# Scan and mixture of adapters on one core: tokens in 4 KB rows over pairs of chunks, transposes in 64-row tiles, a second set of banks in the tail

## The chip, the core and the metric

The kernel runs on one core of a Trainium2 chip. The core has five engines that run their own instruction streams side by side and wait for one another through semaphores: TensorE (PE in the profile; its weight loads are shown as PEld), VectorE (DVE), ScalarE (ACT), GpSimd (POOL) and SyncE (SP), which here only issues transfers. Sixteen DMA engines move data between the device memory and the core's SBUF. TensorE writes into PSUM, which has eight banks of 2 KB per partition; ACT and DVE copy from there. The metric is the device time of one execution in microseconds, the median of several runs.

## The reference

Two layers, one after the other. The first is a linear recurrence over 6400 time steps for 8 sequences of 128 features: `h = a[:, t] * h + b[:, t]`, each h is an output row. Its 51200 rows x then go through a mixture of 8 adapters of rank 16:

```
logits = x @ w_gate                       # 8 experts
topk = two largest; w = softmax over the two
delta[row] += w[row, k] * ((x[row] @ A[e]) @ B[e])   # for its two experts
return x + delta
```

Inputs a and b (26 MB each, fp32) are read once, and the output (26 MB) is written once.

## The kernel before

A *chunk* is 512 tokens; there are 100. In the loads, partition p of a chunk holds the four tokens 4p to 4p+3 (`J` = 4), so one partition's row of a transfer is 4 x 128 x 4 B = 2 KB. Loads bring two chunks at a time (`HC` = 2, 512 KB for a and as much for b, into one of six buffers each), stores take two chunks at a time too; the first four chunks are loaded singly and the last four stored singly.

For each chunk (`front`):

- A and B (L419): four fp32 transposes of a 128x128 tile each, through TensorE against `ident_f`, put a into the bank `pA` and b into one of the two banks `pB`, features on partitions, tokens along the free dimension. The four tokens of a partition go to every fourth column (`"d (p j) -> d j p"`).
- ae (L430): ACT copies pA to SBUF (`a_st`), since the scan may read only one operand from PSUM.
- sc (L442): DVE runs the recurrence over 512 tokens, `xT = a_st * state + pB`, fp16 out. Chunks hang together through the last column of the chunk before; a chunk in which a new sequence begins is done in two pieces.

The rest works in *units* of six blocks of 128 tokens (the last four units have four), 68 units in all (`zlogits` and `back`):

- Z (L462): six matmuls with xT blocks as weights give, per token, 128 adapter values and 8 logits, in the two banks `pZ`; ze (L468) on ACT copies them to `zl`.
- Gating (`gating`, L489 to L518), once for a group of four units (in the tail for groups of 2, 2, 1, 1, 1, 1 units): five small DVE instructions, two sigmoids on ACT and four small POOL instructions give the weights g.
- mu (L533 on POOL, L537 on DVE for the last two units, `MU_DVE` = 2): zw = zl * g, fp16.
- T (L543): six fp16 transposes of zw into the bank `pT`; te (L552 on DVE, for one unit in four L549 on ACT) copies them to `zwT`.
- D (L558, L559): per block two matmuls that add up in the two banks `pO`: x itself (xT against `ident_h`), then zwT against B. oe (L569) on ACT copies to the output buffer `outt` (72 blocks).
- st (L595): SP issues the store when all blocks of its chunks are copied.

So T of a unit waits for te of the unit before (one bank pT), and D waits for oe of the unit before (one pair pO).

The order of instructions on each engine is fixed when the program is made. `Program.schedule` plays a model of the engines with a duration for each operation (such as `0.109 * J` for A), rates for loads and stores (`LOAD_RATE`, `STORE_RATE`), a rank for each operation from `TEMPLATE` and a look-ahead `WINDOW` per engine, and takes, engine by engine, what can start first. `Program.waits` then gives each instruction the semaphore waits that its inputs and buffers need. All loads and stores but one go through SP's queue in the order so planned. WARM transposes on the identity (L359) fill PE in the first microseconds.

Of the kernel before, what the change touches and what calls it, by code (L numbers as in the profile page):

```python
# [10 lines left out]
PERIOD = 6  # L11
# [6 lines left out]
LOAD_RATE = 386e3  # L18
STORE_RATE = 420e3
# [4 lines left out]
WINDOW = {'pe': 22.339, 'act': 15.032, 'dve': 17.853, 'pool': 31.507, 'sp': 21.093}  # L24
# [5 lines left out]
MU_DVE = 2  # L30
WARM0 = 12
WARM = 34
LAST = 2
TEMPLATE = {
    "la": [-13.768, -11.488, -10.699],
    "lb": [-11.599, -10.876, -10.408],
    "A": [-8.739, -5.735, -4.61, -4.527, -4.01, -3.388],
    "B": [-0.753, -0.06, 2.522, 2.886, 3.39, 4.151],
    "ae": [6.378, 8.693, 8.757, 9.146, 10.126, 12.233],
    "sc": [11.891, 15.28, 15.373, 17.047, 17.106, 17.222],  # L40
    "Z": [8.614, 8.864, 13.261, 13.471],
    "ze": [17.232, 19.133, 19.801, 20.09],
    "g1": [13.208],
    "g2": [18.458],
    "g3": [3.74],
    "g4": [5.014],
    "g5": [35.276],
    "g6": [5.048],
    "w1": [11.688],
    "w2": [17.689],  # L50
    "p1": [18.712],
    "p2": [4.238],
    "p3": [33.725],
    "mu": [17.377, 18.243, 18.627, 23.065],
    "T": [19.784, 21.14, 23.513, 25.169],
    "te": [11.814, 12.075, 12.746, 13.615],
    "D": [22.711, 24.793, 26.772, 27.207],
    "oe": [23.268, 23.347, 25.158, 27.374],
    "st": [18.431, 19.751, 20.387],
    "ta": [11.3, 11.673, 14.3, 15.8],  # L60
    "md": [10.222, 11.5, 13.0, 14.5],
    "wu": [-0.392],
    "ch": [5.145],
# [146 lines left out]
def bass_associative_scan_2x2__then__mixture_of_adapters_kernel(  # L210
# [32 lines left out]
    GMAX = 4  # L243
    groups = []
# [14 lines left out]
    NX = 24  # L259
# [13 lines left out]
    with ExitStack() as stack:  # L273
# [19 lines left out]
        a_tm = sbuf("a_tm", [128, HC, J, D], F32, NL)  # L293
        b_tm = sbuf("b_tm", [128, HC, J, D], F32, NL)
        a_st = sbuf("a_st", [128, C], F32, NA)
        xT = sbuf("xT", [128, C], F16, NX)
# [17 lines left out]
        pB = psum("pB", [128, C], F32, 2)  # L314
# [59 lines left out]

        def xblock(b):
            return xT[b // J % NX].rearrange("d (p j) -> d j p", j=J)[:, b % J, :]

# [15 lines left out]

        def load(c, n):
# [3 lines left out]
            for o_l, o_t, key, tile, src in ((o_la, o_A, "la", a_tm, af), (o_lb, o_B, "lb", b_tm, bf)):  # L398
                q = "act" if c == 0 and key == "lb" else "sp"
                op = P.add(  # L400
                    q, f"{key}{c}", n * C * D * 4 / LOAD_RATE, get(o_t, HC * (p - NL) + HC - 1),
                    lambda tile=tile, src=src, q=q: eng[q].dma_start(
                        tile[sl][:, h : h + n, :, :],
                        src[r0 : r0 + n * C, :].rearrange("(h p j) d -> p h j d", p=128, j=J),
                    ),
                    (FIRST, "", 0) if c < 2 else (PERIOD * (c // PERIOD), key, c % PERIOD // 2), sem=dma_sem(f"{key}{sl}" if n == HC else f"{key}x{c % 4}"),
                )
                for k in range(n):
                    o_l[c + k] = op

        def front(c):
            sl = c // HC % NL
            r0 = rows[c]

            def trans(dst, src):
                def f():
                    dv = dst.rearrange("d (p j) -> d j p", j=J)
                    for j in range(J):
                        last = eng["pe"].transpose(dv[:, j, :], src[:, j, :], ident_f[:, :])  # L419
                    return last  # L420
                return f

            o_A[c] = P.add("pe", f"A{c}", 0.109 * J,
                           [(o_la[c], True), (o_id, True)] + get(o_ae, c - 1),
                           trans(pA[:, :], a_tm[sl][:, c % HC, :, :]), fr(c, "A"))
            o_B[c] = P.add("pe", f"B{c}", 0.109 * J,
                           [(o_lb[c], True), (o_id, True)] + get(o_sc, c - 2),
                           trans(pB[c % 2][:, :], b_tm[sl][:, c % HC, :, :]), fr(c, "B"))
# [3 lines left out]
            x = xT[c % NX]  # L432
# [3 lines left out]
            def scan():  # L436
                for s0, s1 in segs:
                    if (r0 + s0) % S == 0:
                        init = 0.0
                    else:  # L440
                        init = xT[(c - 1) % NX][:, C - 1 : C]
                    last = eng["dve"].tensor_tensor_scan(  # L442
                        out=x[:, s0:s1], data0=a_st[c % NA][:, s0:s1], data1=pB[c % 2][:, s0:s1],
# [6 lines left out]
                            + get(xlast, c % NX),  # L450
                            scan, fr(c, "sc"))

        def zlogits(u):
            b0, n = units[u]
            c1 = (b0 + n - 1) // J
# [66 lines left out]
        def back(gi, u):  # L522
# [7 lines left out]
            if u < NU - MU_DVE:  # L530
# [9 lines left out]

            def tr():
                for k in range(n):
                    last = eng["pe"].transpose(pT[:, k * 128 : k * 128 + 128], zw[w][:, k, :], ident_h[:, :])  # L543
                return last

            o_T[u] = P.add("pe", f"T{u}", 0.056 * n, [(o_mu[u], True), (o_ih, True)] + get(o_te, u - 1), tr, ba(gi, u, "T"))
            if te_act(u):
                o_te[u] = P.add("act", f"te{u}", 0.15 + 0.107 * n, [(o_T[u], True)] + get(o_D, u - NW),
                                lambda: eng["act"].copy(zwT[w][:, 0 : n * 128], pT[:, 0 : n * 128]), ba(gi, u, "ta"))  # L549
            else:  # L550
                o_te[u] = P.add("dve", f"te{u}", 0.14 + 0.0672 * n, [(o_T[u], True)] + get(o_D, u - NW),
                                lambda: eng["dve"].tensor_copy(zwT[w][:, 0 : n * 128], pT[:, 0 : n * 128]), ba(gi, u, "te"))  # L552

            def delta():
                for k in range(n):
                    o = k % (n // 2) * 128
                    dst = pO[:, k // (n // 2), o : o + 128]
# [131 lines left out]
```

## Time and profile before

| | |
|---|---|
| median of 3 runs | 208.79 us (208.51 to 209.43) |
| the profiled execution | 209.08 us; from its first to its last instruction (span) 206.9 us |
| granted TensorE clock, mean | 0.992 |
| busy, of the span | PE 94%, DVE 87%, ACT 83%, POOL 64% |
| moved by DMA | 79.17 MB, 383 GB/s over the span |
| the chain that ended last | 88% of it on PE |
| costliest groups | scan L442 120.3 us in 96, mu L533 96.3 us in 66, transposes L419 61.7 us (a) and 61.3 us (b) in 400 each, ae L430 60.5 us in 100 |

A line of an instruction group or of the timeline names the line of the kernel, the engine, the operation, and what is written and read; f16 and f32 are types. Matmuls overlap on PE: one is shown from its start to its end, and the next may start before that. The timeline joins neighbours of one kind (x4). In the table of stages, a row has the stretch in microseconds, its length, then busy time and number of instructions of PE, PEld, DVE, ACT and POOL, then the granted clock, the mean busy share of the 16 DMA engines, and GB/s.

### The profile page before, as it was taken

The numbers are of one execution on the slowest core, as the hardware profiler recorded it, in microseconds if no ns is written. First come the engines' busy times: TensorE is split into PE (matmuls) and PEld (weight loads), VectorE is DVE, ScalarE is ACT, GpSimd is POOL, SyncE is SP. The second block draws the span as 40 slices with busy tenths as digits, with TensorE's granted clock in tenths as the row PEclk, the third lists the DMA queues.
The fourth block names the chain that finished last, engine by engine and source line by source line (L and its number), as shares of the span: only waits on it lengthen the run. The fifth ranks groups of instructions, "written<-read, shape, count | busy, mean of one in ns | idle before, by whom it ended". The sixth has DMA issues, their size and how long they took to land.

```text
span 206.9 us, 6064 instructions
## 1 busy us (share of the span) xinstructions
PE 194.1 (94%) x2434; PEld 185.8 (90%) x2434; DVE 179.2 (87%) x266; ACT 172.5 (83%) x295; POOL 132.8 (64%) x156
## 2 busy tenths in 40 slices
PE   6988699999999999999999999999999999998762
PEld 6976589999999999999999999999999999997641
DVE  0379959999999999999999999999998989978871
ACT  2266949979999999999989898989998989898552
POOL 1000194868686776859594949494959494879960
PEclk9999969999999999999999999999999999999999
DMA  6999999999999999999999999999999999999784
GB/s 195 376 388 385 388 387 387 386 395 399 397 397 400 405 394 403 395 402 403 395 407 398 405 395 404 402 400 406 398 405 400 405 401 401 406 406 389 303 333 159
DMA packets 42251, 79.17 MB, mean 383 GB/s; under 512 B 3696, under 2 KB 3824, under 8 KB 42224
## 3 DMA queue, kind: packets, MB, share of 16 engines
q1 hardware_dynamic: 40752, 78.39, 100.0%
q10 hardware_dynamic: 1472, 0.40, 0.8%
q8 instruction: 19, 0.31, 0.6%
q14 instruction: 8, 0.07, 0.1%
HBM read 52.56 MB, written 26.21 MB: 381 GB/s over the span
## 4 chain that ended last, share of the span: by engine, by line
PE 88%; ACT 4%; DVE 3%; POOL 2%; issue 2%; DVEq 0%; POOLq 0%
PE pB L419 21%; PE pA L419 21%; PE pZ L462 12%; PE pO L558 11%; PE pT L543 10%; PE pO L559 10%; PE pO L359 3%; DVE xT L442 2%; POOL zw L533 1%; ACT zl L468 1%; ACT outt L569 1%; ACT a_st L430 1%; DVE zwT L552 1%; ACT L506 1%; POOL g L518 0%
## 5 line engine op out<-in xcount | busy, mean ns | idle before, releaser
L442 DVE TENSOR_TENSOR_SCAN xT<-a_st,xT,pB 128x512 f16<-128x512 f32 x96 | 120.3, 1253 | 9.1 <-PE pB L419 3.5
L533 POOL TENSOR_TENSOR zw<-zl,g 128x768 f16<-128x768 f32 (+1 forms) x66 | 96.3, 1488 | 1.6
L430 ACT COPY a_st<-pA 128x512 f32<-128x512 f32 x100 | 60.5, 605 | 16.2 <-PE pA L419 14.6
L419 PE MATMUL pA<-ident_f,a_tm 128*128 128x128 f32 x400 | 61.7, 277 | 1.7 <-ACT a_st L430 1.5
L569 ACT COPY outt<-pO 128x768 f32<-128x768 f32 (+1 forms) x68 | 55.0, 808 | 9.3 <-PE pO L559 7.7
L419 PE MATMUL pB<-ident_f,b_tm 128*128 128x128 f32 x400 | 61.3, 279 | 1.2 <-DVE xT L442 1.1
L468 ACT COPY zl<-pZ 128x816 f32<-128x816 f32 (+1 forms) x68 | 57.9, 851 | 2.7 <-PE pZ L462 2.4
L558 PE MATMUL pO<-ident_h,xT 128*128 128x128 f16 x400 | 52.2, 220 | 3.6 <-ACT outt L569 1.5
L559 PE MATMUL pO<-cst_h,zwT 128*128 128x128 f16 x400 | 52.0, 219 | 0.0
L558 PEld LDWEIGHTS pO<-ident_h,xT 128*128 128x128 f16 x400 | 44.5, 113 | 5.4 <-ACT outt L569 2.7
L419 PEld LDWEIGHTS pA<-ident_f,a_tm 128*128 128x128 f32 x400 | 45.3, 143 | 3.8 <-issue 2.2
L419 PEld LDWEIGHTS pB<-ident_f,b_tm 128*128 128x128 f32 x400 | 44.3, 143 | 2.7 <-DVE xT L442 1.5
L501 POOL TENSOR_TENSOR dd<-m 128x24 f32<-128x24 f32 (+2 forms) x21 | 7.0, 333 | 51.2 <-DVE m L499 51.2
L559 PEld LDWEIGHTS pO<-cst_h,zwT 128*128 128x128 f16 x400 | 39.3, 98 | 0.0
L462 PE MATMUL pZ<-cst_h,xT 128*128 128x136 f16 x400 | 35.2, 224 | 0.8 <-DVE xT L442 0.4
L543 PE MATMUL pT<-ident_h,zw 128*128 128x128 f16 x400 | 33.5, 219 | 1.0 <-POOL zw L533 0.9
L552 DVE COPY zwT<-pT 128x768 f16<-128x768 f16 (+1 forms) x53 | 28.1, 530 | 5.0 <-PE pT L543 4.8
L462 PEld LDWEIGHTS pZ<-cst_h,xT 128*128 128x128 f16 x400 | 29.7, 114 | 1.9 <-DVE xT L442 0.9
L543 PEld LDWEIGHTS pT<-ident_h,zw 128*128 128x128 f16 x400 | 26.3, 98 | 2.5 <-POOL zw L533 1.8
L514 POOL TENSOR_TENSOR t<-k,w 128x192 f32<-128x192 f32 (+2 forms) x21 | 9.5, 453 | 11.6 <-ACT w L506 11.2
L442 DVE TENSOR_TENSOR_SCAN xT<-a_st,pB 128x512 f16<-128x512 f32 (+1 forms) x8 | 7.5, 939 | 5.6 <-ACT a_st L430 5.5
L549 ACT COPY zwT<-pT 128x768 f16<-128x768 f16 x15 | 12.2, 815 | 0.0
(22 smaller groups left out, 80.9 us busy)
## 6 DMA issues: line engine op xcount, KB each, us to landing
a_tm<-in_a_dram SPq DMA_DIRECT2D x48, 512.0 KB, 11.2
b_tm<-in_b_dram SPq DMA_DIRECT2D x48, 512.0 KB, 11.2
out_dram<-outt SPq DMA_DIRECT2D x48, 512.0 KB, 11.2
a_tm<-in_a_dram SPq DMA_DIRECT2D x4, 256.0 KB, 4.5
out_dram<-outt SPq DMA_DIRECT2D x4, 256.0 KB, 2.6
b_tm<-in_b_dram SPq DMA_DIRECT2D x3, 256.0 KB, 5.5
b_tm<-in_b_dram ACTq DMA_DIRECT2D x1, 256.0 KB, 3.6
cst_f<-in_moe_A_dram ACTq DMA_DIRECT2D x1, 64.0 KB, 4.5
```

The lines of the kernel that those rows point to most:

```text
L419: last = eng["pe"].transpose(dv[:, j, :], src[:, j, :], ident_f[:, :])
L430: lambda: eng["act"].copy(a_st[c % NA][:, :], pA[:, :]), fr(c, "ae"))
L442: last = eng["dve"].tensor_tensor_scan(out=x[:, s0:s1], data0=a_st[c % NA][:, s0:s1], data1=pB[c % 2][:, s0:s1], initial=init, op0=ALU.mul ...
L462: last = eng["pe"].matmul(pZ[:, k // (n // 2), o : o + W], xblock(b0 + k), Awg_h)
L468: return eng["act"].copy(zl[:, zb : zb + n, :].rearrange("p (h k) w -> p h (k w)", h=2), pZ[:, :, 0 : n // 2 * W])
L533: lambda: eng["pool"].tensor_tensor(out=wv, in0=zv, in1=gv, op=ALU.mult), ba(gi, u, "mu"))
L543: last = eng["pe"].transpose(pT[:, k * 128 : k * 128 + 128], zw[w][:, k, :], ident_h[:, :])
L549: lambda: eng["act"].copy(zwT[w][:, 0 : n * 128], pT[:, 0 : n * 128]), ba(gi, u, "ta"))
L552: lambda: eng["dve"].tensor_copy(zwT[w][:, 0 : n * 128], pT[:, 0 : n * 128]), ba(gi, u, "te"))
L558: eng["pe"].matmul(dst, xblock(b0 + k), ident_h[:, :], start=True, stop=False)
L559: last = eng["pe"].matmul(dst, zwT[w][:, k * 128 : k * 128 + 128], B_h, start=False, stop=True)
L569: return eng["act"].copy(outt[:, o0 : o0 + n, :].rearrange("p (h k) w -> p h (k w)", h=2), pO[:, :, 0 : n // 2 * 128])
```

## The change

- **Pairs.** Chunks are put together to `supers`: four single chunks at the head, then 46 pairs, then four single ones. In a pair, partition p holds the eight tokens 8p to 8p+7 of its 1024, so a partition's row is 4 KB in loads and stores alike. Chunk 0 of the pair lies in partitions 0 to 63, chunk 1 in partitions 64 to 127. xT buffers hold a pair each (12 for 24), and a block of 128 tokens is every eighth column of the pair (`xblock`). A unit's Z waits for both chunks of the pair (`ready`). Stores go by supers, so the four chunks at the head are now stored singly as well.
- **64-row tiles.** A paired chunk is transposed by eight transposes of 64 partitions x 128 features against a 64x64 corner of the identity, for a and for b. One step on PE, P, now issues these of two operands in turn: for an even chunk c, a of chunk c+1 (upper partitions) with b of chunk c (lower ones); for an odd chunk c, b of chunk c with a of chunk c+1, which lies in the next pair. Only at the ends of the row of pairs does a step hold one operand. Unpaired chunks are transposed as before.
- **Tail.** Of the last ten units (`ALT` = 10) every other one uses pA (as fp16) in place of pT and the two banks pB in place of pO. The first of the ten waits for the last ae (its T) and the last two scans (its D). The others wait for te and oe of the unit two before. mu of the units 1, 2, 4, 6, 8 and 10 from the end goes to DVE.
- The model's rates, windows and ranks have other values.

```diff
-LOAD_RATE = 386e3
-STORE_RATE = 420e3
+LOAD_RATE = 396e3
+STORE_RATE = 410e3
...
-MU_DVE = 2
+MU_DVE = [1, 2, 4, 6, 8, 10]
+ALT = 10
...
-LAST = 2
+HALVES = 0.62
+PAIR_RATE = 412e3
+SUP = 2
+SUP_HEAD = [1, 1, 1, 1]
+SUP_TAIL = [1, 1, 1, 1]
...
+    of_chunk = {c0 + k: i for i, (c0, n) in enumerate(supers) for k in range(n)}
+    ready = {b: supers[of_chunk[b // J]][0] + supers[of_chunk[b // J]][1] - 1 for b in range(NBLK)}
...
-    NX = 24
+    NX = 12
...
-        xT = sbuf("xT", [128, C], F16, NX)
+        xT = sbuf("xT", [128, SUP * C], F16, NX)
...
         def xblock(b):
-            return xT[b // J % NX].rearrange("d (p j) -> d j p", j=J)[:, b % J, :]
+            i = of_chunk[b // J]
+            c0, n = supers[i]
+            return xT[i % NX][:, 0 : n * C].rearrange("d (p j) -> d j p", j=n * J)[:, b - c0 * J, :]
...
+        def paired(c):
+            return 0 <= c < NCH and supers[of_chunk[c]][1] == 2
...
+                if paired(c):
+                    view = src[r0 : r0 + n * C, :].rearrange("(p j) d -> p j d", p=128)
+                    dst = tile[sl][:, :, :]
+                else:
+                    view = src[r0 : r0 + n * C, :].rearrange("(h p j) d -> p h j d", p=128, j=J)
+                    dst = tile[sl][:, h * J : (h + n) * J, :].rearrange("p (h j) d -> p h j d", j=J)
...
+        def pieces(c, tile, dst):
+            t = tile[c // HC % NL]
+            h = c % HC
+            if not paired(c):
+                dv = dst.rearrange("d (p j) -> d j p", j=J)
+                return [(dv[:, j, :], t[:, h * J + j, :], ident_f[:, :]) for j in range(J)]
+            dv = dst.rearrange("d (p j) -> d j p", j=HC * J)
+            lo, hi = 64 * h, 64 * h + 64
+            return [(dv[:, j, :], t[lo:hi, j, :], ident_f[lo:hi, lo:hi]) for j in range(HC * J)]
+
+        def trans(*which):
+            def f():
+                lists = [pieces(*w) for w in which]
+                for group in zip(*lists):
+                    for args in group:
+                        last = eng["pe"].transpose(*args)
+                return last
+            return f
...
+            elif c % 2 == 0:
+                if c not in o_A:
+                    o_A[c] = P.add("pe", f"A{c}", HALVES, deps_a(c), trans(part_a(c)), fr(c, "A"))
+                    add_ae(c)
+                o_A[c + 1] = o_B[c] = P.add("pe", f"P{c}", HALVES, deps_a(c + 1) + deps_b(c),
+                                            trans(part_a(c + 1), part_b(c)), fr(c, "B"))
+                add_ae(c + 1)
+            elif paired(c + 1):
+                load_next(c + 1)
+                o_A[c + 1] = o_B[c] = P.add("pe", f"P{c}", HALVES, deps_b(c) + deps_a(c + 1),
+                                            trans(part_b(c), part_a(c + 1)), fr(c, "B"))
+                add_ae(c + 1)
+            else:
+                o_B[c] = P.add("pe", f"B{c}", HALVES, deps_b(c), trans(part_b(c)), fr(c, "B"))
...
-            c1 = (b0 + n - 1) // J
+            c1 = ready[b0 + n - 1]
...
-            if u < NU - MU_DVE:
+            if NU - u not in MU_DVE:
...
+            turn = u - (NU - ALT)
+            po, ptile = pO, pT[:, :]
+            if turn < 0:
+                free_t, free_o = get(o_te, u - 1), get(o_oe, u - 1)
+            elif turn == 0:
+                free_t, free_o = get(o_ae, NCH - 1), get(o_sc, NCH - 1) + get(o_sc, NCH - 2)
+            else:
+                free_t, free_o = get(o_te, u - 2), get(o_oe, u - 2)
+            if turn >= 0 and turn % 2 == 0:
+                po, ptile = pB, pA[:, :].bitcast(F16)
...
-                    out[r0 : r0 + m * C, :].rearrange("(h p j) d -> p h j d", p=128, j=J),
-                    outt[:, q : q + m * J, :].rearrange("p (h j) d -> p h j d", j=J)),
+                    out[r0 : r0 + m * C, :].rearrange("(p j) d -> p j d", p=128),
+                    outt[:, q : q + m * J, :]),
...
```

## The prediction

> **What bounds the kernel now.** I read the page first (busy shares, the forty slices), then the table of stages, the timelines of SP's queue and of PE, and the groups by line and shape.
>
> ```profile
> PE 194.1 (94%) x2434; PEld 185.8 (90%) x2434; DVE 179.2 (87%) x266; ACT 172.5 (83%) x295; POOL 132.8 (64%) x156
> GB/s 195 376 388 385 388 387 387 386 395 399 397 397 400 405 394 403 395 402 403 395 407 398 405 395 404 402 400 406 398 405 400 405 401 401 406 406 389 303 333 159
> ```
>
> Rows of 2 KB move at 387 GB/s while only loads run (slices 3 to 8) and at about 403 once stores are mixed in. The table of stages (PE, PEld, DVE, ACT, POOL, granted clock, share of the DMA engines, GB/s) says when each is full:
>
> ```profile
> 10.00:20.00 10.00, 8.59 (x77) 6.94 (x75) 8.20 (x7) 7.08 (x11) 0.00 (x0) 1.00 1.05 388
> 100.00:120.00 20.00, 20.00 (x271) 19.95 (x270) 19.33 (x26) 18.79 (x33) 15.69 (x16) 1.00 1.05 403
> 190.00:207.00 17.00, 9.63 (x128) 7.14 (x125) 10.07 (x30) 7.91 (x19) 9.54 (x23) 1.00 0.72 272
> ```
>
> A share of 1.05 is a full DMA (packets overlap a little); it holds from 10 to 190 us. SP's queue says the same from the other side: an issue into a queue with room takes 0.37 us, but here each takes the time in which one 512 KB transfer leaves:
>
> ```profile
> 143.49 1.24 SPq L402 DMA_DIRECT2D a_tm<-in_a_dram  x1
> 144.78 1.24 SPq L402 DMA_DIRECT2D b_tm<-in_b_dram  x1
> 146.05 1.28 SPq L595 DMA_DIRECT2D out_dram<-outt  x1
> ```
>
> PE is full at the same time. In its timeline each piece starts where the last one's share ends:
>
> ```profile
> 103.91 0.60 PE L419 MATMUL pA<-ident_f,a_tm 128*128 128x128 f32 x4
> 104.35 0.52 PE L462 MATMUL pZ<-cst_h,xT 128*128 128x136 f16 x6
> 104.70 0.50 PE L543 MATMUL pT<-ident_h,zw 128*128 128x128 f16 x6
> 105.04 0.61 PE L419 MATMUL pB<-ident_f,b_tm 128*128 128x128 f32 x4
> 105.48 0.60 PE L419 MATMUL pA<-ident_f,a_tm 128*128 128x128 f32 x4
> 105.92 0.22 PE L558 MATMUL pO<-ident_h,xT 128*128 128x128 f16 x1
> ```
>
> From start to start: four fp32 transposes 0.44 us (0.109 each), Z of six blocks 0.35, T 0.34, and D 0.67 (the next piece starts at 106.59). The whole of PE's work is 800 x 0.109 + 400 x 0.058 + 400 x 0.056 + 800 x 0.056 = 178 us, and the timeline has no gap of note from 29 to 190 us. Per unit of six blocks PE needs 1.5 x 0.88 + 1.36 = 2.68 us, the DMA (1.18 MB at 403 GB/s) 2.93. So both are limits: PE begins late, works off a backlog, and is done just as the DMA is. Taking away from one alone gains only the tail.
>
> **The change, part by part.**
>
> *Rows of 4 KB.* The trace's packet records give medians of 84 ns for 2048 B, 27 for 512 B and 9 for 4 B: a straight line of 0.0371 ns a byte (57 ns over 1536 B), 76 ns for moving 2 KB and some 9 fixed. By the rates, the pace of one engine is 16 x 2048 B / 387 GB/s = 84.7 ns with loads alone and 81.3 with stores among them, so 8.7 and 5.3 ns are not moving. In the 92 paired chunks 92 x 3 x 262144 / 4096 = 17664 packets go away, 1104 on each engine: 9.6 us at the one price, 5.9 at the other. Loads alone fill 27 of the 188 full microseconds, so 0.14 x 9.6 + 0.86 x 5.9 = 6.4 us, which I take; loads would run at 408 GB/s, the mix at 417. Ends: 0 (the gap to the line is not per packet) and 9.9 (9 ns each).
>
> The Trainium skill, DMA: Bandwidth & Descriptors, section SWDGE vs HWDGE vs iDMA, has a stream of loads with 4 KiB rows at 408.7 GB/s; by that figure an estimate for the loads alone is as above. The same page, section Why small descriptors are slow, puts the fixed price at about three bus cycles a packet; at its 850 MHz that estimates 3.5 ns and 3.9 us saved instead of 6.4.
>
> *Transposes as 64-row tiles.* For 91 steps, eight whole transposes (0.88 us of PE) become 16 of half the rows, each streaming 64 identity columns instead of 128, taken in turn from lower and upper partitions into different banks. No row shows a 64-row matmul. Lower end: half of the fastest pace in the trace (56 ns for 128 fp16 columns), 16 x 0.028 = 0.45 us. Upper end: a half tile costs what a whole one does, 16 x 0.109 = 1.74. The nearest rows are the fp32 transposes themselves. If they are limited by streaming, half the columns cost 0.055, and two halves of the array side by side make that 0.45 in all; if by loading weights, two loads side by side make 0.88. I take the middle, 0.66, so PE is rid of 91 x 0.22 = 20 us. The forecast needs less: PE must be done with the main part 6.4 + 2.5 us earlier, so 0.78 is enough. The 16 pairs also double these instructions (1536 for 800); that is within the ends.
>
> *Waits that pairing adds.* A step P holds B of one chunk and A of the next, so the second B of a pair waits for the next pair's a. From landing to first use, a-loads had 10 us to spare at 70 us and 3 us at 160; one transfer is 1.3. Behind a waiting P stand Z, T and D of older units on PE, and DVE's scan. I cost it at nothing; with the spare gone it is one transfer (1.3 us) now and then, while the DMA is full anyway. A unit's Z now waits for both chunks' scans (1.28 us more); the older xT buffers cover it. Stores and loads keep their number within two issues (0.4 us each of SP, which waits for room).
>
> *Reads at a step of eight.* Z and the first D matmul load xT columns 16 B apart, not 8. Loading takes 98 ns for dense zw and 113 for xT, with the pace 56 to 59 for both. I take 0; 15 ns on each of 800 would be 12 us of PE, still under the 20 freed.
>
> *The tail.* From 190 us the DMA's share is 0.72 of 1.05, so 17 x (1 - 0.72/1.05) = 5.3 us idle, and units come out one by one:
>
> ```profile
> 199.40 0.59 ACT L569 COPY outt<-pO 128x512 f32<-128x512 f32 x1 [0.24 <-PE pO L559]
> 200.78 0.59 ACT L569 COPY outt<-pO 128x512 f32<-128x512 f32 x1 [0.59 <-PE pO L559]
> 202.32 0.59 ACT L569 COPY outt<-pO 128x512 f32<-128x512 f32 x1 [0.96 <-PE pO L559]
> 203.84 0.59 ACT L569 COPY outt<-pO 128x512 f32<-128x512 f32 x1 [0.93 <-PE pO L559]
> ```
>
> About 1.5 us for 256 KB that the DMA stores in 0.65. The second banks let T and D of a unit start beside the copies (0.42 and 0.59) of the one before; four more multiplies (one of 0.69, three of about 1.0) go to DVE, from POOL's 1.06 and 1.5. DVE gets 3.7 us more in 180 to 200 us, where it has 3.9 free. The last store's issue to landing (2.0 us, 0.65 of it moving) can't go, so at most 3.9 is to be had. Against it: the first of the ten units on the second banks waits for the last scan, which ended at 191.7, and its D stood at about 188.3; the 3.4 us are covered while queued stores last, and the units on the old banks can pass. I take 2.5 us off, ends -1 and 3.9.
>
> **Sum.** Span 206.9 - 6.4 - 2.5 = 198.0. The profiled execution took 209.08 for a span of 206.9 (2.2 more) and is 0.3 above the median of 208.79, so 198.0 + 2.2 - 0.3 = 199.9 us, 4.3% less. DVE stays under: 183 us of work from 7 us on ends near 193.
>
> **Rivals.**
>
> *Half tiles at half price, no more (P = 0.88).* For it: no two matmuls in the trace start closer than 55 ns, and 16 x 0.055 = 0.88. Then PE's 178 us stand, it is full from 29 to 190 as now, the DMA's gain shows only as idle DMA, and the tail's 2.5 remains: 206.9 - 2.5 + 1.9 = 206.3 us. Chance 0.11.
>
> *Switching empties the array (slower).* An fp32 transpose takes 277 ns from start to end at a pace of 109. If going from whole to half tiles and back lets the array run empty, each P pays twice the difference, 0.34 us. On top of 0.45 or 0.66 that is 0.79 or 1.00, on top of 0.88 it is 1.22: 91 x (1.22 - 0.88) = 31 us more, 206.9 + 31 - 2.5 + 1.9 = 237 us; with 1.00, 91 x 0.12 = 11 us, 217. It is slower from P = 0.92 on, where 91 x 0.04 eats what tail and offset leave. Against it: the trace goes from fp32 transposes to fp16 matmuls with no gap, but both use the whole array. Chance 0.16, with 1.74 (about 284 us) in it.
>
> The Trainium skill, TensorEngine Tiling (Array Packing), section Key Properties, says that changing the tiling mode drains the engine; no row here shows one, and by that rule this rival's price is due.
>
> *Rows don't matter.* If the full DMA is limited by the bytes alone, 6.4 us are gone from the sum: 206.3 us. Against it: loads alone are slower than the mix, so 387 is not a limit of the memory. Chance 0.07.
>
> **How the numbers follow.** The forecast has 0.66, its own range 195.5 (9.9 and 3.9 saved give 195.0) to 204. A measurement of this kernel tells about 0.5% from no change. Faster by more: forecast 0.66 and most of the two mild rivals, 0.80; within: 0.04; slower: 0.16. The range goes from 195.5 to 207.0, which takes in both mild rivals and leaves out the slower one and a little below.
>
> **What would show it.** Right: P steps at 0.5 to 0.8 us in PE's timeline, PE busy well under 94%, the full DMA at 408 (loads) and 412 to 420 GB/s, packets of 4096 B near 160 ns, last copies closer than 1.5 us. Wrong: PE with no gaps and the DMA's share under 1.05 in mid-kernel (first two rivals); 387 and 403 GB/s again (the third); DVE or POOL full after 185 us with the DMA idle there (the tail).

## The result, and the profile after

| | before | after |
|---|---|---|
| median of 6 runs each, us | 208.56 (208.22 to 209.43) | 212.01 (211.40 to 212.84) |
| the profiled execution, us; span | 209.08; 206.9 | 211.62; 209.8 |
| granted clock, mean | 0.992 | 0.984 |
| last load landed, us | 184.0 | 175.8 |
| output copy of unit 56 ended | 185.3 | 191.0 |
| last output copy ended | 204.4 | 207.1 |

The ratio is 1.0166, with a 95% interval of 1.0132 to 1.0199. The change makes the kernel slower, by 3.5 us; the forecast was 199.9, and its range of 195.5 to 207.0 does not hold the time.

The page's busy shares, rates and granted clock after:

```profile
PE 185.0 (88%) x3170; PEld 165.3 (79%) x3170; DVE 182.0 (87%) x270; ACT 173.7 (83%) x295; POOL 126.6 (60%) x152
PEclk9999999999999999999999999999999999999985
GB/s 196 387 409 408 408 409 409 405 406 412 415 417 414 415 418 409 414 413 416 413 416 410 408 412 411 416 411 415 416 415 409 412 407 399 250 164 169 302 379 102
```

The rows did what the sum said: 408 to 409 GB/s with loads alone, 408 to 418 with stores among them (413 from 60 to 146 us), and the loads are through 8 us sooner. But from slice 35 (178 us) on the DMA has little to move, since the output is not ready. The table of stages shows who is late:

```profile
100.00:120.00 20.00, 18.51 (x347) 16.69 (x345) 18.91 (x28) 18.32 (x31) 13.61 (x15) 1.00 1.02 411
180.00:190.00 10.00, 9.68 (x132) 9.26 (x133) 9.74 (x20) 8.95 (x19) 7.53 (x12) 1.00 0.46 180
200.00:210.00 10.00, 4.70 (x44) 3.48 (x44) 3.95 (x13) 3.06 (x9) 2.42 (x9) 0.65 0.58 224
```

At 180 to 190 us the DMA is used for 0.46 of the time (1.05 before), and DVE and PE are busy for 97% of it. Units do not come sooner; they come later. I measure the pace in mid-kernel from the end of the output copy (oe) of unit 16 to that of unit 40, and give it for four units, for which six chunks are transposed and scanned: 10.79 us before, 11.13 after. At unit 8 the two kernels are level (57.4 and 57.0 us), at unit 56 the new one is 5.7 us behind, and its tail, from there to the last copy, is 3.0 us shorter (16.1 for 19.1). The table of stages from 60 to 146 us, first before, then after:

```profile
60.00:146.00 86.00, 85.99 (x1152) 85.47 (x1150) 82.64 (x114) 80.84 (x136) 62.50 (x65) 1.00 1.05 401
60.00:146.00 86.00, 80.62 (x1492) 72.86 (x1489) 79.60 (x112) 78.59 (x131) 60.12 (x61) 1.00 1.03 413
```

PE is no longer full, and DVE, busy for 82.64 of 86 us before, does less in the same time too.

PE's timeline after, over about one third of a period (start, length; rows of the P steps between the first and the last pair are left out; the last row is the start of the third P step):

```profile
122.71 0.22 PE L634 MATMUL pO<-cst_h,zwT 128*128 128x128 f16 x1
122.86 0.27 PE L455 MATMUL pB<-ident_f,b_tm 64*128 64x64 f32 x1
122.86 0.27 PE L455 MATMUL pA<-ident_f,a_tm 64*128 64x64 f32 x1
122.97 0.22 PE L455 MATMUL pB<-ident_f,b_tm 64*128 64x64 f32 x1
122.97 0.22 PE L455 MATMUL pA<-ident_f,a_tm 64*128 64x64 f32 x1
123.03 0.22 PE L455 MATMUL pB<-ident_f,b_tm 64*128 64x64 f32 x1
...
123.34 0.22 PE L455 MATMUL pA<-ident_f,a_tm 64*128 64x64 f32 x1
124.30 0.27 PE L455 MATMUL pA<-ident_f,a_tm 64*128 64x64 f32 x1 [0.74 <-ACT a_st L473]
124.31 0.27 PE L455 MATMUL pB<-ident_f,b_tm 64*128 64x64 f32 x1
...
124.95 0.51 PE L618 MATMUL pT<-ident_h,zw 128*128 128x128 f16 x6
125.29 0.55 PE L526 MATMUL pZ<-cst_h,xT 128*128 128x136 f16 x6
...
125.85 0.27 PE L455 MATMUL pA<-ident_f,a_tm 64*128 64x64 f32 x1
```

Three things are to be seen. The two halves of a pair start together, and pairs follow at 0.06 us; a P step, from its first start to that of the next piece, takes 0.645 us (124.30 to 124.95), where 0.66 was forecast. Between a whole-array matmul and the first pair lie 150 ns (122.71 to 122.86) in place of 56, so a step costs 0.094 us more on the piece ahead of it, unless that is a P step too; the 0.155 us from the last pair to the next piece are in the 0.645. And once in each period two P steps stand side by side: the second waits for ACT to copy pA out, since there is one bank pA.

Added up over a period (24 blocks, 6 transposing steps of a and b), the starts of pieces on PE give:

| PE, us in a period | before | after |
|---|---|---|
| transposes | 6 x 0.882 = 5.29 | 6 x 0.645 = 3.87 |
| wait of the second P | 0 | 0.80 |
| T | 1.34 | 1.45 |
| Z | 1.42 | 1.79 |
| D | 2.68 | 3.21 |
| sum | 10.73 | 11.12 |

The transposes save 1.42 us, and 1.81 are lost: 0.80 in the wait; 5 x 0.094 = 0.47 in the switches to half tiles, which lie in the times of T, Z and D (the sixth P of a period follows another P); and some 0.54 that remain, nearly all in Z and D. This last part shows in the weight loads (groups by line and shape; busy us, mean ns of one), first before, then after:

```profile
L558 PEld LDWEIGHTS pO<-ident_h,xT 128*128 128x128 f16 x400 | 44.5, 113 | 5.4 <-ACT outt L569 2.7 <-DVE zwT L552 1.4 <-DVE k L503 0.9
L462 PEld LDWEIGHTS pZ<-cst_h,xT 128*128 128x128 f16 x400 | 29.7, 114 | 1.9 <-DVE xT L442 0.9 <-issue 0.6
```

```profile
L633 PEld LDWEIGHTS pO<-ident_h,xT 128*128 128x128 f16 x374 | 46.3, 142 | 3.8 <-DVE zwT L627 2.0 <-ACT outt L644 0.5
L526 PEld LDWEIGHTS pZ<-cst_h,xT 128*128 128x128 f16 x400 | 30.2, 144 | 3.7 <-issue 0.8 <-DVE m L563 0.4 <-DVE xT L506 0.3
L618 PEld LDWEIGHTS pT<-ident_h,zw 128*128 128x128 f16 x374 | 22.6, 98 | 3.3 <-POOL zw L597 1.1 <-DVE zw L601 0.3
```

xT's blocks are now read at every eighth column, 16 B apart, and loading one takes 142 to 144 ns; it took 113 to 114 at every fourth column, and dense zw takes 98. PE's starts in the timeline of D show the pace: mostly 64 ns from a matmul with an xT block to the next and 56 from the other, where both were 56. The first xT block behind a P step takes 113 to 118 ns.

### The profile page after: what moved, and what is told of

The parts are those of the page before. It is cut to its first block, busy times and chain, and to the rows that moved or that the text cites. A ratio compares the mean times of both kernels' runs of the same rounds, so it can differ in the third digit from the quotient of the medians.

```text
span 209.8 us, 7543 instructions
## 1 busy us (share of the span) xinstructions
PE 185.0 (88%) x3170; PEld 165.3 (79%) x3170; DVE 182.0 (87%) x270; ACT 173.7 (83%) x295; POOL 126.6 (60%) x152
## 4 chain that ended last, share of the span: by engine, by line
PE 69%; ACT 15%; DVE 6%; POOL 3%; DMA 2%; issue 2%; ACTq 1%; DVEq 0%
PE pA L455 16%; PE pZ L526 12%; PE pO L633 11%; PE pT L618 10%; PE pB L455 9%; PE pO L634 9%; ACT outt L644 6%; ACT a_st L473 5%; DVE xT L506 3%; DMA cst_f<-in_moe_B_dram 2%; ACT zl L532 2%; ACT zwT L624 1%; DVE L L557 1%; POOL zw L597 1%; POOL t L578 1%
## 5 line engine op out<-in xcount | busy, mean ns | idle before, releaser
L597 POOL TENSOR_TENSOR zw<-zl,g 128x768 f16<-128x768 f32 (+1 forms) x62 | 91.6, 1508 | 1.3
L455 PE MATMUL pA<-ident_f,a_tm 64*128 64x64 f32 (+1 forms) x768 | 70.1, 231 | 12.6 <-ACT a_st L473 12.4
L455 PE MATMUL pB<-ident_f,b_tm 64*128 64x64 f32 (+1 forms) x768 | 69.7, 231 | 1.5 <-DVE xT L506 0.9
L455 PEld LDWEIGHTS pA<-ident_f,a_tm 64*128 64x128 f32 (+1 forms) x768 | 56.2, 139 | 18.5 <-ACT a_st L473 14.0
L455 PEld LDWEIGHTS pB<-ident_f,b_tm 64*128 64x128 f32 (+1 forms) x768 | 56.4, 139 | 7.3 <-issue 1.4
L644 ACT COPY outt<-pO 128x768 f32<-128x768 f32 (+1 forms) x63 | 50.2, 797 | 5.8 <-PE pO L634 5.7
L526 PE MATMUL pZ<-cst_h,xT 128*128 128x136 f16 x400 | 37.8, 230 | 1.0 <-ACT zl L532 0.8
L627 DVE COPY zwT<-pT 128x768 f16<-128x768 f16 (+1 forms) x48 | 25.4, 529 | 0.7 <-PE pT L618 0.7
L618 PEld LDWEIGHTS pT<-ident_h,zw 128*128 128x128 f16 x374 | 22.6, 98 | 3.3 <-POOL zw L597 1.1
L580 POOL TENSOR_TENSOR g<-k,w 128x192 f32<-128x192 f32 (+2 forms) x21 | 9.5, 451 | 4.5 <-ACT w L570 1.3
```

Source lines behind the costliest of these rows:

```text
L455: last = eng["pe"].transpose(*args)
L526: last = eng["pe"].matmul(pZ[:, k // (n // 2), o : o + W], xblock(b0 + k), Awg_h)
L597: lambda: eng["pool"].tensor_tensor(out=wv, in0=zv, in1=gv, op=ALU.mult), ba(gi, u, "mu"))
L618: last = eng["pe"].transpose(ptile[:, k * 128 : k * 128 + 128], zw[w][:, k, :], ident_h[:, :])
L627: lambda: eng["dve"].tensor_copy(zwT[w][:, 0 : n * 128], ptile[:, 0 : n * 128]), ba(gi, u, "te"))
L644: return eng["act"].copy(outt[:, o0 : o0 + n, :].rearrange("p (h k) w -> p h (k w)", h=2), po[:, :, 0 : n // 2 * 128])
```

## The experiments

Each batch was run beside the kernel before, whose median was 208.6 us in each. The pace is that of four units, as above.

| kernel | us | ratio to before | pace | unit 8, us | unit 56, us |
|---|---|---|---|---|---|
| before | 208.56 | 1 | 10.79 | 57.4 | 185.3 |
| after | 212.01 | 1.0166 [1.0132, 1.0199] | 11.13 | 57.0 | 191.0 |
| before, 4 KB rows | 208.44 | 0.9990 [0.9974, 1.0007] | 10.79 | 56.9 | 184.7 |
| before, fewer transposes | 207.82 | 0.9951 [0.9935, 0.9968] | 10.74 | 55.9 | 183.3 |
| before, both | 206.77 | 0.9900 [0.9863, 0.9937] | 10.74 | 57.0 | 183.8 |
| before, both and shorter scans | 201.02 | 0.9637 [0.9622, 0.9651] | 10.05 | 55.6 | 177.0 |
| after, dense xT | 206.96 | 0.9907 [0.9879, 0.9935] | 10.77 | 57.3 | 187.1 |
| after, T moved | 212.36 | 1.0170 [1.0122, 1.0218] | 11.13 | 58.8 | 193.0 |
| after, T moved, dense xT | 207.53 | 0.9949 [0.9928, 0.9969] | 10.80 | 57.3 | 187.5 |
| after, old tail | 213.73 | 1.0253 [1.0232, 1.0274] | 11.13 | 57.1 | 191.1 |
| after, whole transposes | 227.59 | 1.0903 [1.0871, 1.0936] | 12.13 | 62.1 | 207.0 |
| after, planned anew | 209.31 | 1.0025 [1.0002, 1.0048] | 10.68 | 61.9 | 189.7 |
| after, planned anew, dense xT | 207.25 | 0.9936 [0.9908, 0.9964] | 10.58 | 62.8 | 189.1 |
| after, planned anew, fillers | 208.28 | 0.9972 [0.9948, 0.9995] | 10.68 | 62.5 | 190.2 |

The questions were two. Is "the DMA and PE are both limits" the whole truth of the kernel before? And what eats PE's gain in the kernel after?

### The kernel before, freed of one limit after another

*Rows alone.* Loads and stores of pairs get 4 KB rows; tokens of a pair are then mixed up, and all the rest is as before.

```diff
-src[r0 : r0 + n * C, :].rearrange("(h p j) d -> p h j d", p=128, j=J),
+src[r0 : r0 + n * C, :].rearrange("(p h j) d -> p h j d", p=128, j=J),
...
-out[r0 : r0 + m * C, :].rearrange("(h p j) d -> p h j d", p=128, j=J),
+out[r0 : r0 + m * C, :].rearrange("(p h j) d -> p h j d", p=128, j=J),
```

> The kernel before with nothing changed but the rows of the two-chunk loads and stores: eight tokens per partition, 4 KB. Its compute still takes them as four and four, so tokens get mixed up inside a pair; the instructions and their order are those of before. Theory 1 (PE is full from 29 to 190 us and sets the end; the DMA is merely full too): packets go to about 160 ns per 4096 B and the loads to 408 GB/s, but PE's units come at the same 10.7 us per four, and the time stays at 207.5 to 209 us. Theory 2 (the full DMA sets the end): 6.4 us less, about 202 us.

Measured: 208.44 us, no change. In the table of stages the rate rose as it does in the kernel after, and the gain turned into idle DMA near the end:

```profile
100.00:120.00 20.00, 20.00 (x273) 19.97 (x271) 19.29 (x26) 18.83 (x33) 15.34 (x15) 1.00 1.03 416
180.00:190.00 10.00, 9.78 (x139) 9.36 (x137) 8.18 (x22) 9.28 (x19) 8.52 (x13) 1.00 0.60 240
```

So the DMA alone is no limit that can be felt. That much the prediction said ("taking away from one alone gains only the tail").

*Fewer transposes alone.* From chunk 8 on three of the four tiles of a and of b are transposed, so PE is rid of a fourth of that work (12 x 0.109 = 1.3 us of a period, about what the forecast took off).

```diff
-for j in range(J):
+for j in range(J if c < 8 else 3):
```

> The kernel before, with three of the four fp32 transposes of a and of b left out no longer done as four but as three, from chunk 8 on (the fourth quarter of each chunk keeps old values): eight transposes of a chunk become six, 0.65 us of PE for 0.88, which is what a P step of the change takes. Everything else, the planned order too, is as before. Theory 1 (both limits, PE first): the DMA stays full at 400 GB/s and the end moves only by what is idle in the tail and by PE's lead over the DMA, 203 to 207 us. Theory 2 (PE alone): about 20 us less, 189 us. Theory 3 (ACT, DVE or the planned order pace as hard as PE): no change, 208 to 209 us, with waits on PE in place of work.

Measured: 207.82 us, 0.5% less; the pace goes from 10.79 to 10.74. PE's need falls to some 9.4 us, and yet the units hardly come faster. This is near the third theory, a little below its 208 to 209 us.

*Both.*

> Both edits at once: 4 KB rows and six transposes for eight in the kernel before. If the prediction's frame is right (the two limits must both be moved, and then both gains come), 198 to 201 us. If something else paces as hard as these two, 204 to 209 us.

Measured: 206.77 us, 1.0% less. This is the run that decides: both limits that the prediction named are relieved, by as much as it counted on, and 1.8 us come of it where it expected 6.4 from the main part. The table of stages, and the waits from 60 to 150 us (us in total, times, longest):

```profile
100.00:120.00 20.00, 19.28 (x244) 17.76 (x242) 19.26 (x27) 18.77 (x32) 15.34 (x15) 1.00 1.03 416
```

```profile
PEld pB L419 <- DVE xT L442: 6.0, 22, 0.5
```

DVE is busy for 19.26 of 20 us, as it was before (19.33), and PE now waits for the scan to free a bank of pB. This points to DVE as the third limit, right behind the two others; the next run tests it.

*And the scans shortened.* From chunk 32 on a scan ends at column 448 of 512 (the last columns are not computed), which takes an eighth off the costliest work of DVE.

```diff
-segs = list(zip(starts, starts[1:] + [C]))
+segs = list(zip(starts, starts[1:] + [C if c < 32 else 448]))
```

> The kernel before with 4 KB rows, six transposes for eight, and scans of 448 instead of 512 columns from chunk 32 on (the last 64 columns keep old values): DVE has about 0.16 us less in each scan, 0.94 us in a period of six. Theory C (DVE is the third limit, which kept rows and fewer transposes at 206.8): the period falls from 10.73 us to what ACT allows, about 10.1 to 10.3, over 11 periods 5 to 7 us less: 200 to 202 us. Theory D (the planned order keeps the period, whatever the engines' work): 206 to 207 us.

Measured: 201.02 us, 3.6% less, at a pace of 10.05. Shortening the scan on top of the two other reliefs gives 5.75 us more, which is three times what those two give together. So DVE was the third limit, and it was not the planned order that held the pace:

```profile
100.00:120.00 20.00, 19.77 (x265) 18.82 (x263) 19.01 (x30) 19.52 (x35) 15.67 (x17) 1.00 1.03 414
```

All engines but POOL are now above 95% in this stage. The kernel before is balanced to within some per cent between PE, DVE and the DMA, and the change relieves two of the three.

### The kernel after: what eats PE's gain

*Dense reads of xT.* The tokens of a block are taken from 128 neighbouring columns in place of every eighth one (so rows of a pair come out in another order).

```diff
-return xT[i % NX][:, 0 : n * C].rearrange("d (p j) -> d j p", j=n * J)[:, b - c0 * J, :]
+o = (b - c0 * J) * 128
+return xT[i % NX][:, o : o + 128]
```

> The changed kernel, in which Z and the first D matmul of a block read 128 neighbouring columns of xT in place of every eighth (so blocks mix up tokens). Theory A (PE's chain paces the changed kernel, and weights read at a step of 16 bytes are part of it): Z goes back from 63 to 59 ns and D's first matmul from 64 to 56 ns, 0.35 us for a period of four units of 11.13 us; 5 us over the run: 206 to 207.5 us. Theory B (ACT and DVE pace, PE's longer weight loads lie beside their work): 211 to 212.5 us.

Measured: 206.96 us, 5.05 less than the kernel after, and 0.9% under the kernel before. The groups by line and shape:

```profile
L634 PEld LDWEIGHTS pO<-ident_h,xT 128*128 128x128 f16 x374 | 36.0, 98 | 4.4 <-DVE zwT L628 2.6 <-ACT outt L645 0.6
L527 PEld LDWEIGHTS pZ<-cst_h,xT 128*128 128x128 f16 x400 | 24.9, 98 | 3.7 <-issue 0.8 <-DVE L L558 0.5 <-DVE xT L507 0.2
```

A load falls from 142 to 98 ns, and D's starts stand 56 ns apart again. From the starts on PE, D takes 0.23 us less in a period (2.97 for 3.21) and Z 0.16 less (1.63 for 1.79), and the pace fell by 0.36, since PE now waits 0.03 longer for pA. Most blocks of D are 8 ns quicker and most of Z 4; the first block behind a P step, three times a period, is 46 to 50 ns quicker (67 to 70 for 113 to 118). This one line of the change costs more than the whole change loses. The Trainium skill, SBUF — State Buffer, section Door 1: The DMA port swizzle, has a rule that bears on this: SBUF has lines of 16 bytes, reads keep full bandwidth only while at least two of them fall into one line, and each step to a new line pays a penalty. At a step of eight fp16 columns every read meets a line of its own, at a step of four two meet one. The trace agrees only in part: at a step of eight a load takes 142 to 144 ns in place of 98, but at a step of four, where the rule has full bandwidth, it takes 113 to 114 already; and the page's own list, by which two-byte elements can be read at a step of eight for free, is not borne out here. The page gives no size for the penalty.

*T moved between the two P steps.* In the order of PE, where two P and a T follow one another, T now goes between them, so that PE has work while ACT copies pA.

```diff
+pe = P.order["pe"]
+for k in range(len(pe) - 2):
+    if pe[k].name[0] == pe[k + 1].name[0] == "P" and pe[k + 2].name[0] == "T":
+        pe[k + 1], pe[k + 2] = pe[k + 2], pe[k + 1]
+for k, op in enumerate(pe):
+    op.cnt = k + 1
```

> The changed kernel with one thing moved: where its plan has two P steps side by side on PE and a T next (14 times, once a period), T goes between them. In the changed kernel the second P waits 0.8 us there for the copy of the one bank pA, and T takes 0.345. Theory A (the period of 11.13 us is PE's chain: its work of 10.3 us and this wait): 0.345 us less a period, 5 us over the run, 207 to 208 us. Theory B (DVE and ACT pace the period, the wait on PE is slack): 211 to 212.5 us.

> The T moved and xT read at neighbouring columns (tokens mix inside a pair). Theory A, if nothing else paced: another 5 us less, 202 to 203 us. But DVE was busy 96% in the kernel before at a period of 10.7 us. Theory C (DVE is a third limit, at about 10.3 to 10.7 us a period): with the reads alone the period was 10.77, so the T brings at most 0.3 us a period, 203 to 206.5 us, with PE waiting for the scan in place of ae.

Measured: 212.36 us, and 207.53 with dense reads. Neither differs from its counterpart without the swap by more than the runs spread; the gain that the first and the third theory forecast did not come. The waits from 60 to 150 us, first of the kernel after, then with T moved:

```profile
PE pA L455 <- ACT a_st L473: 5.9, 8, 0.7
```

```profile
PE pA L455 <- ACT a_st L473: 2.3, 8, 0.3
PEld pZ L526 <- DVE xT L506: 2.1, 9, 0.2
PEld pB L455 <- issue: 2.3, 9, 0.3
```

The wait did not go; it was cut into three (5.9 against 6.7 in sum), and the pace is the same to the hundredth, 11.13. The starts of the P steps show why (PE's timeline, T moved):

```profile
124.66 0.27 PE L455 MATMUL pB<-ident_f,b_tm 64*128 64x64 f32 x1
126.11 0.27 PE L455 MATMUL pA<-ident_f,a_tm 64*128 64x64 f32 x1 [0.29 <-ACT a_st L473]
127.66 0.24 PE L455 MATMUL pB<-ident_f,b_tm 64*128 64x64 f32 x1
```

Three P steps come close upon one another there. Each fills the one bank pA and must wait until ACT has copied out what the one before it left, so they start 1.45 and 1.55 us apart here as in the kernel after (122.86, 124.30, 125.85), whichever pieces lie between them; the copy before the third P ends at 127.51 here and at 125.70 there. What T gives up at the first wait is waited for again at the next two pieces, Z and the third P. PE waits, but what it waits for is the chain from P over the copy to the next P, and an exchange of neighbours does not shorten that.

*Planned anew.* The planner books a P step at 0.62 us and a block of Z at 0.059 and of D at 0.112. It now gets what the trace shows, with the switch in the P, and ranks and windows are sought anew with these values. An explicit wait is added for the first unit on the second banks.

```diff
+PAIR = 0.74
...
-P.add("pe", f"P{c}", HALVES, deps_a(c + 1) + deps_b(c),
+P.add("pe", f"P{c}", PAIR, deps_a(c + 1) + deps_b(c),
...
-o_Z[u] = P.add("pe", f"Z{u}", 0.059 * n,
+o_Z[u] = P.add("pe", f"Z{u}", 0.0628 * n,
...
-o_T[u] = P.add("pe", f"T{u}", 0.056 * n,
+o_T[u] = P.add("pe", f"T{u}", 0.0572 * n,
...
-o_D[u] = P.add("pe", f"D{u}", 0.112 * n,
+o_D[u] = P.add("pe", f"D{u}", 0.1197 * n,
...
+first = NU - ALT
+o_T[first].deps.append((o_ae[NCH - 1], True))
+o_D[first].deps += [(o_sc[NCH - 1], True), (o_sc[NCH - 2], True)]
```

> The changed kernel with a new order of work. The durations that its planner books for PE are set to what the trace of the changed kernel shows (a P step with its switches 0.74 us for 0.62, a block of Z 0.063 for 0.059, of D 0.120 for 0.112), the ranks and look-aheads were searched anew with them, and the first unit on the second banks is made to wait for the last copies and scans in so many words. The instructions are those of the changed kernel. Theory E (the order, made for a PE that is faster than the real one, costs the changed kernel its 0.8 us of waiting a period): the period falls from 11.13 to 10.7 to 10.9, 206 to 208 us, which beats both kernels by a little. Theory F (PE's own work and the chain from P over the copy of a to the next P set the period, whatever the order): 210.5 to 212.5 us.

> The newly ordered kernel with xT read at neighbouring columns (tokens mix inside a pair). If PE still paces it, another 0.35 us a period and 3 to 5 us in all; if DVE's 10.7 paces it by now, 1 us or less below the newly ordered one.

Measured: 209.31 us, 2.7 less than the kernel after and level with the kernel before; 207.25 with dense reads. The table of stages in mid-kernel:

```profile
100.00:120.00 20.00, 19.81 (x365) 17.62 (x362) 19.14 (x28) 18.69 (x33) 14.41 (x17) 1.00 1.03 415
```

PE has hardly a gap left, DVE is at 19.14, and the pace is 10.68, better than before (10.79). So both losses, the wait and the strided reads, can be undone one without the other, and either alone brings the pace to 10.7 (10.68 and 10.77). Both together bring 10.58, and not the 10.3 that their sizes would sum to: there PE and DVE are busy for 19.49 of 20 us each from 100 to 120 us. That fits DVE as the next limit, as in the kernel before, though no scan was shortened here to show it.

The pace is as the first theory has it, the time is not (206 to 208 us). The new order begins later: unit 8 is done at 61.9 us in place of 57.0, and at unit 56 it is ahead by only 1.3 us (189.7 for 191.0). More of its gain comes from the tail: 12.1 us from unit 56 to the last copy for 16.1, of which 1.4 are lost again between the last copy and the end of the span (4.1 us for 2.7). So the 2.7 us are not the worth of the wait alone, and how much of them the measured durations brought and how much the new search, no run separates. On top of dense reads the new order brings nothing (207.25 us, 206.96 without it). The profiled execution, at 207.73 us, is the fastest of ten, and eight of them took 209.08 to 209.67. In the table of stages of the replanned kernel the granted clock falls early on:

```profile
20.00:24.00 4.00, 2.47 (x46) 2.09 (x46) 3.94 (x7) 2.91 (x5) 0.24 (x1) 1.00 1.03 410
24.00:28.00 4.00, 2.31 (x38) 2.06 (x38) 2.73 (x4) 2.78 (x6) 2.44 (x4) 0.63 1.03 408
28.00:32.00 4.00, 4.00 (x49) 3.36 (x48) 2.86 (x5) 2.48 (x5) 3.92 (x4) 0.52 1.03 410
```

*Planned anew, with fillers.* To hold the clock up, 29 more transposes of the identity go where PE waited between 19 and 28 us.

```diff
+for at, n in (("P8", 3), ("P10", 6), ("Z5", 5), ("P12", 12), ("Z6", 3)):
+    k = [op.name for op in pe].index(at)
+    pe[k:k] = [P.add("pe", f"wv{at}{i}", 0.109, [(o_id, True)],
+                     lambda: eng["pe"].transpose(pO[:, 0, 0:128], ident_f[:, :], ident_f[:, :]), START)
+               for i in range(n)]
```

> The replanned order of the changed kernel, with 29 more transposes of the identity (like the WARM ones; into a bank that nothing has read or written for the result yet) put on TensorE where it waited between 19 and 28 us. Why: the replanned kernel is at its 8th unit (end of the output copy) at 61.9 us, the changed kernel at 57.0, although its steady pace is better (21.4 us for 8 units against 22.25). Theory 1, the clock: in the replanned kernel the granted clock falls to 0.63 at 24 to 28 us and 0.52 at 28 to 32 us, behind waits of 0.8, 0.6 and 1.7 us, where the changed kernel's plan has WARM transposes (20.8 to 24.9 us) and keeps 1.00. By it the clock stays at 1.00 from 20 to 40 us, the 8th unit comes at 57 to 59 us and the time falls by 2 to 4 us, to 205.5 to 207.5 us, below both kernels. Theory 2, the order itself: the units begin late because the plan puts the chunks' steps first; then the clock rises, the 8th unit stays near 61 us, and the time stays within 0.5% of 209.3 us.

Measured: 208.28 us, ratio 0.9972 (0.9948 to 0.9995). From 24 us on the clock is at 1.00; before, from 20 to 24 us, it is now lower than without the fillers (0.71 for 1.00):

```profile
20.00:24.00 4.00, 4.00 (x56) 3.14 (x56) 2.90 (x6) 2.54 (x4) 0.00 (x0) 0.71 1.02 409
24.00:28.00 4.00, 3.62 (x55) 3.18 (x51) 3.46 (x5) 3.42 (x6) 1.26 (x3) 1.00 1.03 409
28.00:32.00 4.00, 3.70 (x69) 3.21 (x69) 3.05 (x4) 2.67 (x5) 3.84 (x5) 1.00 1.03 410
```

Unit 8 stays at 62.5 us, so its lateness is the order's and not the clock's, as the second theory has it. The time fell by 1.0 us, less than the 2 to 4 of the first theory and more than nothing (the two intervals just miss each other); the two profiled executions, of 207.73 and 208.46 us, do not show where. This is the best kernel here that does the whole work: 3.7 us under the kernel after, and level with the kernel before to within half a per cent.

### Two parts of the change by themselves

*The old tail.* No second banks, and the multiplies of the last two units on DVE as before.

```diff
-MU_DVE = [1, 2, 4, 6, 8, 10]
-ALT = 10
+MU_DVE = [1, 2]
+ALT = -1
```

> The changed kernel without the second set of banks and with the multiplies of the last two units alone on DVE, as before the change. By the times of the last copies, the new tail makes up about 2 us from unit 56 to the end (22.6 us for 24.8): without it 213.5 to 215 us. If the first of the ten units, which waits for the last scan, costs as much as the banks save: 211.5 to 212.5 us.

Measured: 213.73 us, 1.7 more than the kernel after; from unit 56 to the last copy 18.2 us against 16.1. The new tail is a gain, at two thirds of the forecast 2.5. Its last copies are still not close (timeline of ACT, kernel after):

```profile
200.70 0.58 ACT L644 COPY outt<-pB 128x512 f32<-128x512 f32 x1 [0.58 <-PE pB L634]
202.41 0.59 ACT L644 COPY outt<-pO 128x512 f32<-128x512 f32 x1 [0.45 <-PE pO L634]
205.70 0.58 ACT L644 COPY outt<-pB 128x512 f32<-128x512 f32 x1 [2.70 <-PE pB L634]
206.56 0.58 ACT L644 COPY outt<-pO 128x512 f32<-128x512 f32 x1 [0.27 <-PE pO L634]
```

One gap of 2.7 us is left, in the ten microseconds in which the granted clock is 0.65. The timeline shows what lies in it (after):

```profile
202.72 1.32 DVE L601 TENSOR_TENSOR zw<-zl,g 128x512 f16<-128x512 f32 x2 [0.94 <-POOL g L582]
203.50 0.61 PE L618 MATMUL pA<-ident_h,zw 128*128 128x128 f16 x4 [1.12 <-DVE zw L601]
```

DVE waits 0.94 us for the gate of the last units, PE waits 1.12 us for DVE's multiply, and the matmuls of D that follow start about 105 ns apart (204.62 to 205.46 for eight) in place of 56. So the gap begins with the gating, and the lower clock adds to it; what each is worth was not tried.

*Whole transposes.* Each P issues eight whole 128-row transposes in place of 16 halves, all else as in the kernel after (tokens of a pair are mixed up).

```diff
-if not paired(c):
+if True:
     dv = dst.rearrange("d (p j) -> d j p", j=J)
```

> The changed kernel with eight whole 128-row transposes in each P step in place of sixteen of 64 rows (the tokens of a pair get mixed), all else as it was: a P step takes 0.88 us, with no change of tile size, for 0.645 and 0.094 on the piece ahead. If PE's chain sets the period, 6 x 0.14 = 0.86 us a period more, 12.0 us, and 13 us in all: 223 to 227 us; that would be the worth of the 64-row tiles inside this change. If the period is set elsewhere, 212 to 215.

Measured: 227.59 us, 15.6 more, at a pace of 12.13. The half tiles are worth this much inside the change, switches included: without them PE is busy for 19.22 of 20 us from 100 to 120 us and DVE for 17.43. The time is a little above the forecast 227, whose 6 x 0.14 counts six switches a period where there are five.

## Why the prediction was wrong, point by point

- **"So both are limits": the step that failed first.** The stage from 100 to 120 us was in the prediction with DVE at 19.33 of 20 us, and was read for PE and the DMA alone. DVE was then put off with a sum over the span ("183 us of work from 7 us on ends near 193"). That sum supposes that DVE never waits, and in a chain of engines it does: from 60 to 146 us it was idle for 3.4 of 86 us before and for 6.4 after. The runs on the kernel before show the size: both reliefs without the change's own costs give 1.8 us, and a shorter scan on top of them 5.75. Against a third limit at 97% the forecast 6.4 us was not to be had, whatever P cost. These runs put what was to be had near 207 us (206.77 for both reliefs, 206.96 and 207.25 for the dense kernels).
- **"I take 0; 15 ns on each of 800 would be 12 us of PE, still under the 20 freed": the second step that failed.** The loads grew by 29 ns, the pace by 8 (D) and 4 (Z), and by 46 to 50 behind a P step, and this cost 5 us. The cover that I named, PE's freed time, did not exist: once the wait and the switches were paid, PE had nothing free. The row for it stood in the trace (98 against 113 ns at a step of four), and it pointed up; I read it as flat because the pace had not moved yet.
- **P at 0.66 us**: 0.645 in place, and for five of six 0.094 on the piece ahead, 0.74 together. Under the 0.78 that I called enough, and still not enough, since the 0.78 allowed for nothing else on PE.
- **Switching empties the array**: the price is 0.094 us in and 0.095 out, 0.19 together and not 0.34. The Trainium skill, TensorEngine Tiling (Array Packing), section Key Properties, says that changing the mode drains the engine; the trace agrees in that a change costs time (150 and 155 ns between starts, for 56 and 61 without a change), at about half the price that I took from an fp32 transpose's 277 ns from start to end. The rival fell: P was to be 0.92 or more for it.
- **Waits that pairing adds, costed at nothing**: I looked for late loads, and in mid-kernel PE waits for none. The wait that came was for ACT's copy of the one bank pA, 0.80 us a period. It is not pairing as such that makes it but the order: the plan, which books P at 0.62 us, puts two side by side, and the second must wait for the copy. The order planned anew has no two P side by side and no such wait of note, and is 2.7 us faster, its shorter tail included.
- **Rows of 4 KB**: 408 and 417 GB/s forecast, 408 to 409 and 408 to 418 measured; packets of 4096 B take 159 ns (160 forecast). The rate was right and its 6.4 us were not worth anything, as the run with rows alone says. The third rival, that rows don't matter, had 206.3 for another reason (bytes as the limit), which the rates refute. With these rows a full DMA shows a share of 1.03 (416 GB/s in the run with rows alone), so a share under 1.05 in mid-kernel could not have been the sign of being wrong that I took it for.
- **The tail**: 2.5 us forecast, 1.7 measured. The wait of the first unit on the second banks, which the prediction priced at up to 3.4 us and the description of the change names, is not in the program: when that unit is made, the last chunks' copies and scans do not exist yet, and the lookup (`get`) finds nothing. Nothing waited there. In the profiled execution its T starts at 188.8 us and its D at 190.2, after the last copy of pA (186.0) and the last scan (187.5) had ended, so the missing wait neither cost time nor did harm there.
- **The slower rival** had the right sign and the wrong mechanism. None of the rivals was what happened: half tiles that hold their price, in a kernel whose next limit leaves 1.0% to be had, with a strided read on the engine that was to be relieved.

## What to carry to other kernels

Before a gain is summed up, list every engine's busy share in the stage that counts, not over the span: an engine at 97% there is a limit, and relieving its neighbours is worth what is left up to it. When a layout is changed to please the DMA, follow the new stride to every reader, weight loads above all, and give the price to the engine as if it had no slack. And when durations change, give the measured ones to whatever plans the order: the order planned anew, with 0.74 us for P in place of 0.62, was 2.7 us faster, more than the new tail's 1.7, though no run shows which part of that the durations brought.

## What the runs showed of the hardware

- Loading a 128-column fp16 weight block takes 98 ns dense, 113 at every fourth column and 142 to 144 at every eighth; the pace of the matmuls that use them moves only at the last (56 to 64 ns in D), most of all in the first block behind a P step (113 to 118 ns, 67 to 70 with dense reads).
- Two 64-row transposes on the two halves of the array start, in most steps, within 10 ns of each other and pairs follow at 61 to 62 ns, against 109 ns for one whole fp32 transpose. Going from whole to half tiles costs 94 ns, going back 95.
- The granted clock can fall behind short waits of PE: in the order planned anew, with PE busy for 2.47 of 4 us from 20 to 24 us, it was 0.63 and then 0.52 in the next two stretches of 4 us, and with fillers it was 1.00 there. The busy share alone does not say when: in the kernel after PE was busy for 2.31 of 4 us from 12 to 16 us, and the clock stayed at 1.00.
